# Batch 1's front in the first y phase, regrouped: grouped h tiles, kv and x in one piece each, v1 loaded ahead of the last two w_out rows, and both transpose halves in one PSUM tile

## The chip, the cores and the metric

The kernel runs on one core of a Trainium2 chip. TensorE does its matmuls and transposes and writes the results into a memory called PSUM; VectorE and ScalarE copy them out of it ("evacuate" them), and with GpSimd they convert ("cast") loaded data to bfloat16. The metric is the device time of one execution in microseconds (us), of which less is better. All runs counted here were fast, that is, within 1.5% of the fastest run of their kernel. The profile's span, from the first to the last instruction, is some 1.8 us shorter than the device time (279.9 for 281.66).

## The reference, cut to what matters

```python
# attention without a square matrix, per batch (8) and head (8); seq 576, head size 64
q_s = softmax(q, over head_dim)
k_s = softmax(k, over seq)
kv  = einsum('bhsd,bhse->bhde', k_s, v)
x   = einsum('bhsd,bhde->bhse', q_s, kv)        # -> (4608 tokens, 512)
# then a feed-forward layer with an exact Gelu
h = x @ w_in                                     # 512 -> 2048
out = gelu(h) @ w_out                            # 2048 -> 512
```

Everything is float32 outside; the kernel computes its matmuls in bfloat16.

## The kernel before

The kernel goes through the batches. For each there are five kinds of TensorE work: transposes of the normalised q ("tp"), kv, x, the "h phase" (x times w_in, 16 tiles t of 4 matmuls, each followed by a Gelu on ScalarE), and the "y phase" (Gelu times w_out, 4 token groups j times 16 rows t). The front of batch 1 (tp, kv, x) is fitted in at the end of batch 0's y phase. Up to this point the loads stream in on one queue: q, k, v of batch 0, then w_in in five blocks and w_out in four, with q and k of batch 1 ahead of the last w_out block and v of batch 1 ("v1") behind it.

The kernel's PSUM buffers are three of one bank with tag "h", two "y", one "a", and one of two banks, "a2".

```python
psum_h = tile_pool(bufs=3); psum_y = tile_pool(bufs=2); psum_a = tile_pool(bufs=1)   # in PSUM

def tp_mm(b, half):
    ...
    pool, tag = (psum_h, "h") if half == 1 else (psum_a, "a")
    ps = pool.tile([128, J, 2, 128], BF16, tag=tag)          # one bank each
    st[b][f"tp{half}"] = ps
    ...  # 8 transposes into ps

def tp_step(b, half):
    tp_mm(b, half)
    tp_evac(b, half)                                          # copy to SBUF, VectorE

# loads, all on one queue, in this order
wi = [load_wi(i) for i in range(5)]
wo = [load_wo(i) for i in range(3)]
load_main(1, "q", q, 2)
load_pair(1, "k", k, 2)
wo.append(load_wo(3, 2))                                      # two halves of 512 KB
load_pair(1, "v", v, 4)                                       # four of 288 KB

h_phase(0, {...casts...}, groups={0: 2})       # t=0,1 as a pair, then t by t
...
cast_wo(3, wo[3], 0, 2)                        # VectorE
cast_wo(3, wo[3], 2, 2)                        # VectorE
for hp in range(3):
    cast_v(1, hp, nc.gpsimd)
for t in range(12):
    for j in range(J):
        y_mm(0, yps[j], j, t)
tp_step(1, 0)
tp_step(1, 1)
cast_v(1, 3)                                   # VectorE
load(3)
for t in (12, 13):
    for j in range(J):
        y_mm(0, yps[j], j, t)
kv_mm(1, 0); kv_norm(1, 0, 1)
y_end(0); y_end(1)                             # y_end(j): rows 14 and 15 of group j
y_out(0, yps[0], 0)
x_tile(1, 0, psum_a, "a"); x_tile(1, 1, psum_h, "h")
x_mm(1, 0)
kv_mm(1, 1)
x_evac(1, 0, "s"); x_evac(1, 1, "s")           # "s": ScalarE
kv_norm(1, 1, 2)
y_out(0, yps[1], 1)
y_end(2); y_end(3)
xx = psum_a.tile([128, 2, M], FP32, tag="a2", name="xx")
st[1]["x2"], st[1]["x3"] = xx[:, 0], xx[:, 1]
x_mm(1, 1)
x_evac(1, 2)                                   # VectorE
x_evac(1, 3, "s")                              # ScalarE
...
h_phase(1, ...)
# [...] batches 2 to 7 and the rest follow
```

The softmax here doesn't subtract the row's maximum and nothing guards it: scores larger than these inputs give would overflow.

Of the kernel before, what the change touches and what calls it, by code (L numbers as in the profile page):

```python
# [8 lines left out]
FP32 = mybir.dt.float32  # L9
BF16 = mybir.dt.bfloat16  # L10
# [6 lines left out]
def kernel(  # L17
# [16 lines left out]
    nc = tc.nc  # L34
# [3 lines left out]
    J = 4  # L38
    M = 128 * J
    R = S - M  # L40
    HP = H // 2
    NDM = DM // 128
# [20 lines left out]
    wo_bf = singles.tile([128, NDF, DM], BF16)  # L63
# [17 lines left out]
    st = [dict() for _ in range(B + 1)]  # L81
# [10 lines left out]
    def load_pair(b, name, t, parts=1):  # L92
        f = f32in.tile([128, HP, NS * D], FP32, tag=name + "f")
        st[b][name + "f"] = f
        src = t[b].rearrange("h (p n) d -> (h p) (n d)", n=NS).rearrange("(x q) f -> q x f", q=128)
        n = HP // parts
        for i in range(parts):
            nc.sync.dma_start(out=f[:, i * n:(i + 1) * n, :], in_=src[:, i * n:(i + 1) * n, :])  # L98

    def load(b):  # L100
        load_main(b, "q", q)
        load_pair(b, "k", k)
        load_pair(b, "v", v)
# [40 lines left out]
    def cast_v(b, hp, eng=nc.vector):  # L144
        eng.tensor_copy(  # L145
            out=v_aug[b % 2][:, hp, :, 0:D],
            in_=st[b]["vf"][:, hp, :].rearrange("p (n d) -> p n d", n=NS),
        )
# [5 lines left out]
    def kv_mm(b, half):  # L154


        if "kv" not in st[b]:
            st[b]["kv"] = psum_a.tile([128, 2, 2, 256], FP32, tag="a2", name="kv")
        ps = st[b]["kv"]
        for n in range(NS):  # L160
            for i in range(2):
                for hh in range(2):
                    hp = 2 * half + i
                    pr = slice(hh * 64, hh * 64 + 64)
                    c = slice((hh ^ i) * 64, (hh ^ i) * 64 + 64)
                    nc.tensor.matmul(  # L166
                        ps[c, i, half, 0:D + 1], ek[b % 2][pr, hp, n, :],
                        v_aug[b % 2][pr, hp, n, 0:D + 1], start=(n == 0), stop=(n == NS - 1),
                    )

    def kv_norm(b, h0, h1):

        ps = st[b]["kv"]
        m = h1 - h0
        rec = small.tile([128, 2, 2], FP32, tag="reck")
        nc.vector.reciprocal(rec[:, :, 0:m], ps[:, :, h0:h1, D])
        nc.vector.tensor_tensor(  # L177
            out=kvc[b].rearrange("p (h i) d -> p i h d", i=2)[:, :, h0:h1],
            in0=ps[:, :, h0:h1, 0:D],
            in1=rec[:, :, 0:m].unsqueeze(3).to_broadcast([128, 2, m, D]), op=ALU.mult,  # L180
        )

    def kv_step(b):
        kv_mm(b, 0)
        kv_mm(b, 1)
        kv_norm(b, 0, 2)
# [16 lines left out]
    def tp_mm(b, half):  # L203
        if half == 0:
            st[b]["qT"] = attn_sb.tile([128, J, HP, 128], BF16, tag="qT", name="qT")
        pool, tag = (psum_h, "h") if half == 1 else (psum_a, "a")
        ps = pool.tile([128, J, 2, 128], BF16, tag=tag)
        st[b][f"tp{half}"] = ps
        for i in range(2):
            hp = 2 * half + i  # L210
            for j in range(J):
                nc.tensor.transpose(
                    ps[:, j, i, :],
                    st[b]["eq"][:, j, 2 * hp:2 * hp + 2, :].rearrange("p h d -> p (h d)"),
                    identity,
                )
# [19 lines left out]
    def x_tile(b, hp, pool, tag):  # L236
        if "xT" not in st[b]:
            st[b]["xT"] = attn_sb.tile([128, HP, M], BF16, tag="xT", name="xT")
        st[b][f"x{hp}"] = pool.tile([128, M], FP32, tag=tag, name="ps")
# [32 lines left out]
    def x_evac(b, hp, eng="v"):  # L272
        ps = st[b][f"x{hp}"]
        if eng == "v":
            nc.vector.tensor_copy(out=st[b]["xT"][:, hp, :], in_=ps)  # L275
        else:
            nc.scalar.copy(out=st[b]["xT"][:, hp, :], in_=ps)  # L277

    def h_phase(c, ins, groups={}, pre={}):


        g = moe_sb.tile([128, NDF, M], BF16, tag="g", bufs=1)
        st[c]["g"] = g
        xT = st[c]["xT"]
        t1 = 0
        while t1 < NDF:
            t0, t1 = t1, t1 + groups.get(t1, 1)
            ts = range(t0, t1)
            pss = [psum_h.tile([128, M], FP32, tag="h", name="ps") for t in ts]
            for dm in range(NDM):  # L290
                if t0 == 0:
                    for f in pre.get(dm, []):
                        f()
                for ps, t in zip(pss, ts):
                    nc.tensor.matmul(  # L295
                        ps, wi_bf[:, dm, t * 128:(t + 1) * 128], xT[:, dm, :],
                        start=(dm == 0), stop=(dm == NDM - 1),
                    )
            for ps, t in zip(pss, ts):
                nc.scalar.activation(out=g[:, t, :], in_=ps, func=AF.Gelu)  # L300
                for f in ins.get(t, []):
                    f()

    def y_mm(c, ps, j, t):
        nc.tensor.matmul(  # L305
            ps, st[c]["g"][:, t, j * 128:(j + 1) * 128], wo_bf[:, t, :],
            start=(t == 0), stop=(t == NDF - 1),
        )

    def y_out(c, ps, j):  # L310
        y_sb = moe_sb.tile([128, DM], FP32, tag="y_sb")
        nc.vector.tensor_copy(out=y_sb, in_=ps)  # L312
        if c < B:
            dst = out[c * S:c * S + M, :].rearrange("(p j) n -> p j n", j=J)[:, j, :]
            nc.sync.dma_start(out=dst, in_=y_sb)
        else:
            for b2 in range(2):
                r0 = (2 * j + b2) * S + M
                nc.sync.dma_start(out=out[r0:r0 + R, :], in_=y_sb[b2 * R:(b2 + 1) * R, :])
# [48 lines left out]
    def cast_wi(i, w, eng):  # L368
        n = wi_cols[i]
        r = n // 128  # L370
        o = wi_bf[:, :, wi_off[i]:wi_off[i] + n].rearrange("p d (c m) -> p d c m", c=r)
        w = w[:, :, 0:n].rearrange("p d (m c) -> p d c m", c=r)
        if eng == "p":
            for h in range(2):
                nc.gpsimd.tensor_copy(out=o[:, 2 * h:2 * h + 2], in_=w[:, 2 * h:2 * h + 2])
        else:
            d = NDM // wi_parts[i]
            for c in range(0, NDM, d):
                nc.vector.tensor_copy(out=o[:, c:c + d], in_=w[:, c:c + d])  # L379

    def load_wo(i, parts=1):
        w = wst.tile([128, 4, DM], FP32, tag="w")
        src = moe_w_out[i * 512:(i + 1) * 512, :]
        if i == 0:
            for h in range(2):
                nc.sync.dma_start(
                    out=w[:, 2 * h:2 * h + 2],
                    in_=src[256 * h:256 * h + 256].rearrange("(p c) f -> p c f", c=2),
                )
            return w  # L390
        src = src.rearrange("(p c) f -> p c f", c=4)
        n = 4 // parts
        for h in range(parts):
            nc.sync.dma_start(out=w[:, h * n:(h + 1) * n], in_=src[:, h * n:(h + 1) * n])
        return w

    def cast_wo(i, w, c0=0, n=4):
        nc.vector.tensor_copy(  # L398
            out=wo_bf[:, 4 * i + c0:4 * i + c0 + n, :], in_=w[:, c0:c0 + n]
        )  # L400

    def warm(n, z=zeros):
        ps = psum_y.tile([128, DM], FP32, tag="y")
# [26 lines left out]
    wo = [load_wo(i) for i in range(3)]  # L430
    load_main(1, "q", q, 2)
    load_pair(1, "k", k, 2)
    wo.append(load_wo(3, 2))
    load_pair(1, "v", v, 4)
    load(2)
    nc.vector.memset(zeros32, 0.0)  # L436
    nc.vector.memset(zeros, 0.0)
# [20 lines left out]
    for hp, pool, tag in ((0, psum_y, "y"), (1, psum_y, "y"), (2, psum_a, "a"), (3, psum_h, "h")):  # L458
# [16 lines left out]
        6: [lambda: cast_wi(4, wi[4], "v")],  # L475
        9: [lambda: cast_wo(0, wo[0])],
        12: [lambda: cast_wo(1, wo[1])],
    }, groups={0: 2})


    exp_q(1, parts=2)
# [5 lines left out]
    norm_q(1, 0, 2)  # L487
    norm_q(1, 1, 2, nc.vector)
    cast_wo(3, wo[3], 0, 2)
    cast_wo(3, wo[3], 2, 2)  # L490
    for hp in range(3):
        cast_v(1, hp, nc.gpsimd)
    for t in range(12):
        for j in range(J):
            y_mm(0, yps[j], j, t)
    tp_step(1, 0)
    tp_step(1, 1)
    cast_v(1, 3)
    load(3)
    for t in (12, 13):  # L500
        for j in range(J):
            y_mm(0, yps[j], j, t)

    def y_end(j):
        for t in (14, 15):
            y_mm(0, yps[j], j, t)

    kv_mm(1, 0)
    kv_norm(1, 0, 1)
    y_end(0)  # L510
    y_end(1)
    y_out(0, yps[0], 0)
    x_tile(1, 0, psum_a, "a")
    x_tile(1, 1, psum_h, "h")
    x_mm(1, 0)
    kv_mm(1, 1)
    x_evac(1, 0, "s")
    x_evac(1, 1, "s")
    kv_norm(1, 1, 2)
    y_out(0, yps[1], 1)  # L520
    y_end(2)
    y_end(3)
    xx = psum_a.tile([128, 2, M], FP32, tag="a2", name="xx")
    st[1]["x2"], st[1]["x3"] = xx[:, 0], xx[:, 1]
    x_mm(1, 1)
    x_evac(1, 2)
    x_evac(1, 3, "s")
    y_out(0, yps[2], 2)
    y_out(0, yps[3], 3)
    h_phase(1, {12: [lambda: cast_v_all(2)]}, groups={0: 2})  # L530
# [79 lines left out]
```

## Time and profile before

| | before |
|---|---|
| device time, median of the first 3 runs (us) | 281.54 |
| TensorE busy, share of the span | 97% |
| h phase of batch 0, start to start of y (us) | 15.04 |
| first transpose of batch 1 to its h phase (us) | 6.08 |
| h phase of batch 1 (us) | 14.00 |
| the same phase undisturbed, batch 2 (us) | 13.82 |

The tables and sums of this document go by the starts of TensorE's pieces in the timeline: the start of one piece less the start of the one before. The recorded lengths of the pieces run into one another, because the profile models the ends of matmuls. Two more figures of the kernel before: GpSimd begins its three casts of v1 at 40.52, after a wait for the load, and an undisturbed h phase (batch 2) starts at 76.23 and its y phase at 90.05, so it takes 13.82 us. The lines of "before" on which the main readings rest are in the prediction below.

### The profile page before, as it was taken

The numbers are of one execution on the slowest core, as the hardware profiler recorded it, in microseconds if no ns is written. First come the engines' busy times: TensorE is split into PE (matmuls) and PEld (weight loads), VectorE is DVE, ScalarE is ACT, GpSimd is POOL, SyncE is SP. The second block draws the span as 40 slices with busy tenths as digits, with TensorE's granted clock in tenths as the row PEclk, the third lists the DMA queues.
The fourth block names the chain that finished last, engine by engine and source line by source line (L and its number), as shares of the span: only waits on it lengthen the run. The fifth ranks groups of instructions, "written<-read, shape, count | busy, mean of one in ns | idle before, by whom it ended". The sixth has DMA issues, their size and how long they took to land.

```text
span 279.9 us, 4557 instructions
## 1 busy us (share of the span) xinstructions
PE 271.2 (97%) x1922; PEld 125.6 (45%) x1922; DVE 102.5 (37%) x150; ACT 156.8 (56%) x242; POOL 32.9 (12%) x25
## 2 busy tenths in 40 slices
PE   7689999999999999999999999999999999999995
PEld 3334454444444444444444444444444444444443
DVE  3757496309763530084007500552005200230012
ACT  5756663689466915692469436853683264036400
POOL 1530040002020140005000500050005000000000
PEclk9999999999999999999999999999999999999999
DMA  7999999961994129801991189126501500120033
GB/s 231 385 404 429 399 402 406 400 249 52 283 388 70 40 83 263 332 38 51 237 369 60 40 201 370 67 77 173 129 0 75 150 2 0 75 77 0 0 77 76
DMA packets 44852, 50.10 MB, mean 179 GB/s; under 512 B 20384, under 2 KB 29856, under 8 KB 44576
## 3 DMA queue, kind: packets, MB, share of 16 engines
q1 hardware_dynamic: 44544, 49.68, 53.4%
q8 instruction: 15, 0.25, 0.4%
q10 hardware_dynamic: 288, 0.13, 0.2%
q14 instruction: 5, 0.04, 0.1%
HBM read 36.70 MB, written 9.44 MB: 165 GB/s over the span
## 4 chain that ended last, share of the span: by engine, by line
PE 75%; DMA 20%; ACT 2%; SPq 1%; DVE 0%; ACTq 0%; issue 0%
PE ps L305 36%; PE ps L295 35%; DMA w<-in_moe_w_in_dram 6%; DMA f<-in_k_dram 5%; DMA f<-in_v_dram 4%; DMA out_dram<-y_sb 3%; DMA touch<-in_moe_w_out_dram 2%; PE kv L166 1%; PE ps L327 1%; PE ps L251 1%; ACT ek L138 1%; ACT e L133 1%; ACTq L423 0%; ACT L133 0%; SPq L98 0%; DVE v_aug L145 0%
## 5 line engine op out<-in xcount | busy, mean ns | idle before, releaser
L295 PE MATMUL ps<-xT,wi_bf 128*128 128x512 bf16 x576 | 126.1, 379 | 1.1 <-DVE wi_bf L379 1.0
L305 PE MATMUL ps<-wo_bf,g 128*128 128x512 bf16 x560 | 124.2, 379 | 0.0
L300 ACT ACTIVATE g<-ps 128x512 bf16<-128x512 f32 x144 | 85.6, 597 | 68.5 <-PE ps L295 68.5
L295 PEld LDWEIGHTS <-wi_bf 128*128 128x128 bf16 x576 | 56.1, 98 | 69.4 <-DVE wi_bf L379 1.5
L305 PEld LDWEIGHTS <-g 128*128 128x128 bf16 x560 | 53.9, 98 | 64.3 <-issue 0.4
L312 DVE COPY y_sb<-ps 128x512 f32<-128x512 f32 x35 | 23.9, 686 | 80.6 <-PE ps L305 80.2
L198 POOL TENSOR_TENSOR e<-e,recq 128x2048 bf16<-128x2048 bf16 (+1 forms) x9 | 25.7, 2856 | 177.8 <-DVE recq L197 149.5
L145 DVE CAST v_aug<-f 128x576 bf16<-128x576 f32 x26 | 17.9, 746 | 47.6 <-DMA f<-in_v_dram 47.6
L277 ACT CAST xT<-ps 128x512 bf16<-128x512 f32 x19 | 10.2, 589 | 30.0 <-PE ps L251 20.4
L196 DVE TENSOR_REDUCE qsum<-e 128x16 f32<-128x1024 bf16 (+1 forms) x13 | 21.0, 1615 | 14.8 <-ACT e L133 14.8
L133 ACT ACTIVATE e<-f 128x512 bf16<-128x512 f32 (+1 forms) x42 | 20.5, 556 | 2.0 <-DMA f<-in_q_dram 1.7
L138 ACT ACTIVATE ek<-f 128x2304 bf16<-128x2304 f32 (+1 forms) x10 | 17.2, 1730 | 1.7 <-DMA f<-in_k_dram 1.7
L275 DVE CAST xT<-ps 128x512 bf16<-128x512 f32 x15 | 9.7, 686 | 17.7 <-PE ps L251 14.8
L79 ACT ACT_TABLE_LOAD x9 | 11.5, 1283 | 2.8 <-issue 2.6
L133 ACT ACT_TABLE_LOAD x7 | 9.0, 1283 | 0.1
L405 PE MATMUL ps<-zeros 128*128 128x512 f32 (+1 forms) x14 | 7.6, 686 | 1.5 <-DVE zeros L436 1.5
L379 DVE CAST wi_bf<-w 128x512 bf16<-128x512 f32 (+1 forms) x8 | 7.1, 910 | 2.8 <-DMA w<-in_moe_w_in_dram 2.6
L166 PEld LDWEIGHTS <-ek 64*64 64x64 bf16 x576 | 6.5, 105 | 2.9 <-issue 1.1
L166 PE MATMUL kv<-v_aug,ek 64*64 64x65 bf16 x576 | 7.1, 193 | 0.1
L398 DVE CAST wo_bf<-w 128x2048 bf16<-128x2048 f32 (+1 forms) x5 | 5.1, 1011 | 4.1 <-DMA w<-in_moe_w_out_dram 4.1
L198 DVE TENSOR_TENSOR e<-e,recq 128x1024 bf16<-128x1024 bf16 x4 | 6.4, 1608 | 0.1
L251 PE MATMUL ps<-qT,kvc 64*64 64x512 bf16 x60 | 5.0, 390 | 1.0 <-DVE kvc L177 1.0
(33 smaller groups left out, 41.4 us busy)
## 6 DMA issues: line engine op xcount, KB each, us to landing
out_dram<-y_sb SPq DMA_DIRECT2D x32, 256.0 KB, 2.3
f<-in_k_dram SPq DMA_DIRECT2D x6, 1152.0 KB, 9.8
f<-in_v_dram SPq DMA_DIRECT2D x6, 1152.0 KB, 11.8
f<-in_q_dram SPq DMA_DIRECT2D x6, 1024.0 KB, 7.3
w<-in_moe_w_in_dram SPq DMA_DIRECT2D x6, 512.0 KB, 8.9
f<-in_k_dram SPq DMA_DIRECT2D x4, 576.0 KB, 10.0
f<-in_v_dram SPq DMA_DIRECT2D x8, 288.0 KB, 7.5
f<-in_q_dram SPq DMA_DIRECT2D x4, 512.0 KB, 8.6
```

Of the source, the lines that this page charges most:

```text
L79: nc.scalar.activation(out=scr[:, 1:2], in_=scr[:, 0:1], func=func)
L133: nc.scalar.activation(out=dst[:, i], in_=src[:, u], func=AF.Exp)
L138: nc.scalar.activation(out=ek[b % 2][:, i:i + n], in_=st[b]["kf"][:, i:i + n].rearrange("p x (n d) -> p x n d", n=NS), func=AF.Exp,)
L145: eng.tensor_copy(out=v_aug[b % 2][:, hp, :, 0:D], in_=st[b]["vf"][:, hp, :].rearrange("p (n d) -> p n d", n=NS),)
L166: nc.tensor.matmul(ps[c, i, half, 0:D + 1], ek[b % 2][pr, hp, n, :], v_aug[b % 2][pr, hp, n, 0:D + 1], start=(n == 0), stop=(n == NS - 1),)
L196: nc.vector.reduce_sum(out=qsum, in_=eq[:, :, hs, :], axis=AX.X)
L198: eng.tensor_tensor(out=eq[:, :, hs, :], in0=eq[:, :, hs, :], in1=recq.unsqueeze(3).to_broadcast([128, J, w, D]), op=ALU.mult,)
L277: nc.scalar.copy(out=st[b]["xT"][:, hp, :], in_=ps)
L295: nc.tensor.matmul(ps, wi_bf[:, dm, t * 128:(t + 1) * 128], xT[:, dm, :], start=(dm == 0), stop=(dm == NDM - 1),)
L300: nc.scalar.activation(out=g[:, t, :], in_=ps, func=AF.Gelu)
L305: nc.tensor.matmul(ps, st[c]["g"][:, t, j * 128:(j + 1) * 128], wo_bf[:, t, :], start=(t == 0), stop=(t == NDF - 1),)
L312: nc.vector.tensor_copy(out=y_sb, in_=ps)
```

## The change

The intent: fewer switches between kinds of TensorE work at batch 1's front, v1 early enough for kv in one go, w_out's last rows off VectorE, and no wait for a late cast of w_in in batch 0.

```diff
@@ tp_mm
-        pool, tag = (psum_h, "h") if half == 1 else (psum_a, "a")
-        ps = pool.tile([128, J, 2, 128], BF16, tag=tag)
+        if b == 1:
+            if half == 0:
+                st[b]["tp"] = psum_a.tile([128, 2, J, 2, 128], BF16, tag="a2", name="tp")
+            ps = st[b]["tp"][:, half]
+        else:
+            pool, tag = (psum_h, "h") if half == 1 else (psum_a, "a")
+            ps = pool.tile([128, J, 2, 128], BF16, tag=tag)
@@ h_phase: tiles named in ybanks take one of y's banks
-            pss = [psum_h.tile([128, M], FP32, tag="h", name="ps") for t in ts]
+            pss = []
+            for t in ts:
+                pool, tag = (psum_y, "y") if t in ybanks else (psum_h, "h")
+                pss.append(pool.tile([128, M], FP32, tag=tag, name="ps"))
@@ cast_wi: one cast for each of the four rows, in all blocks
-            d = NDM // wi_parts[i]
-            for c in range(0, NDM, d):
-                nc.vector.tensor_copy(out=o[:, c:c + d], in_=w[:, c:c + d])
+            for c in range(NDM):
+                nc.vector.tensor_copy(out=o[:, c], in_=w[:, c])
[...]
@@ loads
-    wo.append(load_wo(3, 2))
+    wo.append(load_wo(3))            # now its first two rows only
     load_pair(1, "v", v, 4)
+    load_wo_end(wo[3])               # its last two rows, one by one
@@ batch 0
-    }, groups={0: 2})
+    }, groups={0: 2, 4: 4}, ybanks=(6, 8))
@@ batch 1's front
-    cast_wo(3, wo[3], 2, 2)          # VectorE
     [...]
     tp_step(1, 0)
     tp_step(1, 1)
     cast_v(1, 3)
     load(3)
-    [... the order shown above ...]
+    cast_wo(3, wo[3], 2, 1, "s")     # ScalarE
+    y_part(12, range(J))
+    y_part(13, range(J))
+    kv_step(1)                       # both halves, one normalisation
+    cast_wo(3, wo[3], 3, 1, "s")     # ScalarE
+    y_part(14, range(J))
+    y_part(15, (0, 1))
+    y_out(0, yps[0], 0)
+    y_out(0, yps[1], 1)
+    x_tile(1, 0, psum_a, "a")
+    x_tile(1, 1, psum_h, "h")
+    xx = psum_a.tile([128, 2, M], FP32, tag="a2", name="xx")
+    st[1]["x2"], st[1]["x3"] = xx[:, 0], xx[:, 1]
+    x_mm(1, 0)
+    x_mm(1, 1)
+    x_evac(1, 0, "s")
+    x_evac(1, 1, "s")
+    x_evac(1, 2)                     # VectorE
+    x_evac(1, 3)                     # VectorE
+    y_part(15, (2, 3))
     [...]
```

More of the change, by code (lines that the diff above doesn't have):

```diff
@@ L277, in x_evac, with h_phase @@
             nc.scalar.copy(out=st[b]["xT"][:, hp, :], in_=ps)
-    def h_phase(c, ins, groups={}, pre={}):
+    def h_phase(c, ins, groups={}, ybanks=()):
         g = moe_sb.tile([128, NDF, M], BF16, tag="g", bufs=1)
@@ L288, in h_phase @@
             ts = range(t0, t1)
-            pss = [psum_h.tile([128, M], FP32, tag="h", name="ps") for t in ts]
+            pss = []
+            for t in ts:
+                pool, tag = (psum_y, "y") if t in ybanks else (psum_h, "h")
+                pss.append(pool.tile([128, M], FP32, tag=tag, name="ps"))
             for dm in range(NDM):
-                if t0 == 0:
-                    for f in pre.get(dm, []):
-                        f()
                 for ps, t in zip(pss, ts):
@@ L376, in cast_wi, with load_wo @@
         else:
-            d = NDM // wi_parts[i]
-            for c in range(0, NDM, d):
-                nc.vector.tensor_copy(out=o[:, c:c + d], in_=w[:, c:c + d])
-    def load_wo(i, parts=1):
+            for c in range(NDM):
+                nc.vector.tensor_copy(out=o[:, c], in_=w[:, c])
+    def load_wo(i):
         w = wst.tile([128, 4, DM], FP32, tag="w")
@@ L391, in load_wo, with load_wo_end, cast_wo @@
         src = src.rearrange("(p c) f -> p c f", c=4)
-        n = 4 // parts
-        for h in range(parts):
-            nc.sync.dma_start(out=w[:, h * n:(h + 1) * n], in_=src[:, h * n:(h + 1) * n])
-        return w
-    def cast_wo(i, w, c0=0, n=4):
-        nc.vector.tensor_copy(
-            out=wo_bf[:, 4 * i + c0:4 * i + c0 + n, :], in_=w[:, c0:c0 + n]
-        )
+        if i == 3:
+            nc.sync.dma_start(out=w[:, 0:2], in_=src[:, 0:2])
+            return w
+        nc.sync.dma_start(out=w, in_=src)
+        return w
+    def load_wo_end(w):
+        src = moe_w_out[3 * 512:4 * 512, :].rearrange("(p c) f -> p c f", c=4)
+        for c in (2, 3):
+            nc.sync.dma_start(out=w[:, c], in_=src[:, c])
+    def cast_wo(i, w, c0=0, n=4, eng="v"):
+        o, w = wo_bf[:, 4 * i + c0:4 * i + c0 + n, :], w[:, c0:c0 + n]
+        if eng == "v":
+            nc.vector.tensor_copy(out=o, in_=w)
+        else:
+            nc.scalar.copy(out=o, in_=w)
     def warm(n, z=zeros):
@@ L489, with y_part @@
     cast_wo(3, wo[3], 0, 2)
-    cast_wo(3, wo[3], 2, 2)
     for hp in range(3):
         cast_v(1, hp, nc.gpsimd)
+    def y_part(t, js):
+        for j in js:
+            y_mm(0, yps[j], j, t)
     for t in range(12):
-        for j in range(J):
-            y_mm(0, yps[j], j, t)
+        y_part(t, range(J))
     tp_step(1, 0)
@@ L499 @@
     load(3)
-    for t in (12, 13):
-        for j in range(J):
-            y_mm(0, yps[j], j, t)
-    def y_end(j):
-        for t in (14, 15):
-            y_mm(0, yps[j], j, t)
-    kv_mm(1, 0)
-    kv_norm(1, 0, 1)
-    y_end(0)
-    y_end(1)
+    cast_wo(3, wo[3], 2, 1, "s")
[5 more added lines that the diff above has]
+    y_part(15, (0, 1))
     y_out(0, yps[0], 0)
+    y_out(0, yps[1], 1)
     x_tile(1, 0, psum_a, "a")
     x_tile(1, 1, psum_h, "h")
+    xx = psum_a.tile([128, 2, M], FP32, tag="a2", name="xx")
+    st[1]["x2"], st[1]["x3"] = xx[:, 0], xx[:, 1]
     x_mm(1, 0)
-    kv_mm(1, 1)
+    x_mm(1, 1)
     x_evac(1, 0, "s")
     x_evac(1, 1, "s")
-    kv_norm(1, 1, 2)
-    y_out(0, yps[1], 1)
-    y_end(2)
-    y_end(3)
-    xx = psum_a.tile([128, 2, M], FP32, tag="a2", name="xx")
-    st[1]["x2"], st[1]["x3"] = xx[:, 0], xx[:, 1]
-    x_mm(1, 1)
     x_evac(1, 2)
-    x_evac(1, 3, "s")
+    x_evac(1, 3)
+    y_part(15, (2, 3))
     y_out(0, yps[2], 2)
```

## The prediction

> **What bounds the kernel now.** I first read the page's busy shares, then the timeline of each engine for the first 92 us (the change touches nothing later), then the sources and tiles concerned.
>
> ```profile
> PE 271.2 (97%) x1922; PEld 125.6 (45%) x1922; DVE 102.5 (37%) x150; ACT 156.8 (56%) x242; POOL 32.9 (12%) x25
> ```
>
> TensorE is busy 97% of the span, so only stretches where it stands still, or does more than it must, can give time back. The scale comes from its timeline:
>
> ```profile
> 14.63 4.28 PE L295 MATMUL ps<-xT,wi_bf 128*128 128x512 bf16 x19
> 19.95 9.89 PE L295 MATMUL ps<-xT,wi_bf 128*128 128x512 bf16 x45 [1.04 <-DVE wi_bf L379]
> 29.67 10.52 PE L305 MATMUL ps<-wo_bf,g 128*128 128x512 bf16 x48
> 40.03 1.06 PE L212 MATMUL ps<-identity,e 128*128 128x128 bf16 x16
> 40.92 1.89 PE L305 MATMUL ps<-wo_bf,g 128*128 128x512 bf16 x8
> 42.74 0.48 PE L166 MATMUL kv<-v_aug,ek 64*64 64x65 bf16 x36
> 43.16 1.04 PE L305 MATMUL ps<-wo_bf,g 128*128 128x512 bf16 x4
> 44.12 0.41 PE L251 MATMUL ps<-qT,kvc 64*64 64x512 bf16 x4
> 44.36 0.51 PE L166 MATMUL kv<-v_aug,ek 64*64 64x65 bf16 x36
> 44.80 1.04 PE L305 MATMUL ps<-wo_bf,g 128*128 128x512 bf16 x4
> 45.77 0.41 PE L251 MATMUL xx<-qT,kvc 64*64 64x512 bf16 x4
> 46.11 14.16 PE L295 MATMUL ps<-xT,wi_bf 128*128 128x512 bf16 x64
> ```
>
> Columns: start, length, engine, line, instruction, count, idle time before and what ended it. I use start to start. The 48 matmuls from 29.67 to 40.03 take 0.216 us each, 64 take 13.82. One real gap stands between 14.63 and 46.11: 1.04 us at about 18.9, where tile t=4 of batch 0's h phase needs the fourth row of the third w_in block. From 40.03 to 46.11 there is none: 6.08 us of transposes, y, kv and x matmuls, closely packed. Batch 1's v does not hold TensorE up. So the change can win at most about 1 us at the first place and some tenths at the second, of 281.54: under 0.6%.
>
> VectorE's timeline says what ended the gap, and when the next block comes:
>
> ```profile
> 19.28 0.61 DVE L379 CAST wi_bf<-w 128x512 bf16<-128x512 f32 x1 [1.31 <-DMA w<-in_moe_w_in_dram]
> 20.51 2.33 DVE L379 CAST wi_bf<-w 128x1024 bf16<-128x1024 f32 x2 [0.62 <-DMA w<-in_moe_w_in_dram]
> ```
>
> The cast waits for the load, so the stage is fed at DMA speed; the stretch table gives 414 GB/s and a DMA share of 1.04 there. Two casts of 1.08 in 2.33 mean that the second began about 21.76, when its half landed.
>
> The line that decides my forecast stands in the second place, in the timelines of VectorE and ScalarE:
>
> ```profile
> 46.23 0.69 DVE L275 CAST xT<-xx 128x512 bf16<-128x512 f32 x1 [0.20 <-PE xx L251]
> ...
> 46.96 0.59 ACT L277 CAST xT<-xx 128x512 bf16<-128x512 f32 x1 [1.31 <-DVE xT L275]
> ```
>
> The two evacuations read different halves of one two-bank PSUM tile, xx; yet ScalarE began only 0.04 after VectorE ended (46.92). Elsewhere, where each x has its own PSUM tile, VectorE and ScalarE read side by side (73.54 and 73.32) and write the same xT. So it is sharing the PSUM tile that puts the two engines in a row.
>
> **What the Trainium skill says.** "PSUM — Partial Sum Buffer", section "PSUM bank collisions raise a hardware error": two engines must not access one bank and quadrant together, while different banks run clean. The wait on xx is thus no need of the chip, if the halves are the two banks that their sizes say; the trace shows that the program waits all the same. "TensorEngine Tiling (Array Packing)", section "Key Properties": changing the tiling mode drains TensorE. The trace agrees: four y matmuls after kv take 0.96 (43.16 to 44.12) instead of 0.86, eight after the transposes 1.82 instead of 1.73, so about 0.1 a return. "ScalarE: Activation LUTs", section "Table sets: the hidden batching unit": plain copies are in every table set. The trace agrees: at 44.58 ScalarE casts under the Gelu table with no load of a table. The same page, section "What ACT_TABLE_LOAD costs", gives 186 ns + 0.833 per element, so 0.61 us for 512; the trace's casts from PSUM take 0.59.
>
> **The change part by part.**
>
> *h phase of batch 0: four t in one group, one and then t=8 in y's banks.* t=0 to 3 end on TensorE at about 18.09 (14.63 + 16 x 0.216). Then come 12 matmuls (three rows for four t), 2.6 us, before the late fourth row is needed, and its cast is done at 19.89: the 1.04 gap goes. The fourth of the group (t=7) takes the bank of t=3, whose Gelu ends at 18.89, so about 0.2 is lost there; the group ends at about 21.76 (18.95 + 13 x 0.216). Then t=8 needs all rows of the fourth block. Its casts become four of 0.61, some 0.55 apart: rows 2 and 3 land at 21.76 and are cast at 22.37 and 22.92. t=8's last matmul starts at about 22.97 instead of unhindered at 22.4. After it come 28 more: 22.97 + 29 x 0.216 = 29.24. The fifth block is cast by about 25.4, and t=12 wants it at 25.8. Against 29.67: **-0.43**. The rest of the gap moves to the next block, because the load did not get faster.
>
> *v1 ahead of the last two w_out rows, ScalarE casting these.* Rows for t=12, 13 as before. v1 lands some 512 KB / 0.4 = 1.3 us earlier (POOL's first v cast at about 39.2, not 40.52), the last quarter at about 41.4. The w_out rows land at about 42.0 and 42.6, are cast by about 43.3, and are used after 43.9 and 44.8 by the sums below. ScalarE is idle then (4.63 us before 44.58). VectorE loses one cast of 0.69. Off the path: **0**.
>
> *kv, then y 14 and 15, then x, each in one go.* Durations from undisturbed places: kv x72 0.74 (73.32 to 74.06), x x8 0.46 (99.85 to 100.31). After the transposes: y x8 1.82, kv 0.74, y x6 1.30 + 0.10, x 0.46, y x2 0.43 + 0.10 = 4.95. Before: 46.11 - 40.92 = 5.19. **-0.24**: one return to full mode fewer, and joined kv and x.
>
> *The transposes of batch 1 in one two-bank tile a2.* Before, the halves had two PSUM tiles, and 16 transposes took 0.89. Now the first half is written, VectorE reads it, and the second half is written into the same tile. If TensorE is held as ScalarE was on xx, it waits for the whole evacuation. From the first transpose: eight start within 0.39, the last lasts 0.22, VectorE starts at 0.65 (40.03 to 40.68 before), takes 0.69, TensorE goes on at about 1.38 instead of 0.445. **+0.94** on the path, as every later matmul queues behind.
>
> *x evacuation against the next h phase.* Let x start at X. ScalarE has x0 at X + 1.05 and x1 at X + 1.53 (as 44.12 led to 44.58 and 1.07 of work). VectorE first takes two y tiles, from X - 0.1, then x2 and x3, each 0.61 apart: x3 ready at X + 2.42. The first matmul needing it would be ready at X + 0.99 + 6 x 0.216 = X + 2.29: a wait of 0.19 with hand-over. Before, 64 matmuls took 14.00 there instead of 13.84, so 0.16 was lost already. **+0.03**.
>
> Sum: -0.43 - 0.24 + 0.94 + 0.03 = **+0.30**, so 281.84; I say 281.8.
>
> **The rivals.** *No wait on the shared tile*: TensorE writes bank two while VectorE reads bank one. For it: nothing on the chip forbids that, and whoever made the tile may have meant it. Against it: the wait of ScalarE on xx. Then the sum is -0.64: 280.9. *The gap disappears whole*, if VectorE's finer casts keep pace or the loads land a little earlier: a further 0.5 less, so 281.3, or 280.4 with the first rival; against it speaks that the load is at 414 GB/s already. *The w_out rows or v1 come late*: the margin of the last cast is over 1 us when transposes stall, and some 0.6 when they don't; 2 KB runs instead of 4 KB may slow the loads, and every us of that beyond the margin shows in full: 282 to 283. *The gain in front is hidden by the loads of batch 1*: exp of q1 starts when its load lands (33.06, 1.31 idle), whatever TensorE did. But the normalised q is ready at 38.97, and the transposes would start at 39.6, so 0.6 is to spare.
>
> **Range and chances.** I give the shared-tile wait five chances in six, so 281.8 is the centre, and the range must still reach the other outcome: 280.8 to 282.2. Every route stays within 1% of 281.54, hence almost all chance on "within 2%".
>
> **What would show it.** In TensorE's timeline of the changed kernel: no wait at t=4, a wait of some 0.5 for the wi_bf cast at t=8, and y of batch 0 starting at about 29.24. The transposes as two groups of eight, with some 0.9 idle between them whose releaser is VectorE's qT copy (wrong if 16 run together). kv as one piece of 72 near 43.2, h of batch 1 near 46.3. ScalarE casting wo_bf twice, each about 0.6, with TensorE waiting for neither. After 60 us the pattern of before, shifted by +0.3. I would be wrong, above all, if the halves of the shared tile were not held apart.

## The result, and the profile after

The changed kernel took 281.89 us (median of 6 runs, 281.34 to 283.15), the one before 281.61 (6 runs, 281.27 to 282.06). The ratio is 1.0011, with a 95% interval of 0.9989 to 1.0033. A ratio here is the mean time of one kernel's fast runs over the mean of the other's in the same rounds, so not quite the ratio of the medians. The totals alone say only that the two are equal within their noise. The traces say why.

TensorE's timeline of the changed kernel, in the columns start, length, engine, line, instruction, count, and in brackets the idle time before it and what ended that (the "releaser"). Line numbers have moved: L300 is the h matmul, L310 y, L217 the transposes, L256 x.

```profile
14.75 14.70 PE L300 MATMUL ps<-xT,wi_bf 128*128 128x512 bf16 x64
29.29 10.52 PE L310 MATMUL ps<-wo_bf,g 128*128 128x512 bf16 x48
39.65 0.61 PE L217 MATMUL tp<-identity,e 128*128 128x128 bf16 x8
41.05 0.61 PE L217 MATMUL tp<-identity,e 128*128 128x128 bf16 x8 [0.78 <-DVE qT L226]
41.49 1.89 PE L310 MATMUL ps<-wo_bf,g 128*128 128x512 bf16 x8
43.31 0.78 PE L166 MATMUL kv<-v_aug,ek 64*64 64x65 bf16 x72
44.02 1.47 PE L310 MATMUL ps<-wo_bf,g 128*128 128x512 bf16 x6
45.42 0.41 PE L256 MATMUL ps<-qT,kvc 64*64 64x512 bf16 x4
45.66 0.39 PE L256 MATMUL xx<-qT,kvc 64*64 64x512 bf16 x4
45.98 0.60 PE L310 MATMUL ps<-wo_bf,g 128*128 128x512 bf16 x2
46.51 14.03 PE L300 MATMUL ps<-xT,wi_bf 128*128 128x512 bf16 x64
60.38 6.42 PE L310 MATMUL ps<-wo_bf,g 128*128 128x512 bf16 x29
```

The reader is to see three things. The 1.04 gap of the first line of before is gone, and y starts 14.54 after h instead of 15.04. The transposes are two pieces now, with 0.78 idle between them and VectorE's qT copy named as what ended it; from the first of them to h it is 6.86 instead of 6.08. And kv and x are one piece each.

VectorE's and ScalarE's parts of it:

```profile
40.30 0.69 DVE L226 COPY qT<-tp 128x1024 bf16<-128x1024 bf16 x1 [0.66 <-PE tp L217]
41.69 0.69 DVE L226 COPY qT<-tp 128x1024 bf16<-128x1024 bf16 x1 [0.70 <-PE tp L217]
42.30 0.74 DVE L145 CAST v_aug<-f 128x576 bf16<-128x576 f32 x1
```

```profile
42.12 1.24 ACT L412 CAST wo_bf<-w 128x512 bf16<-128x512 f32 x2 [2.13 <-DMA w<-in_moe_w_out_dram]
```

TensorE starts its second half at 41.05, when VectorE's first copy has ended (40.30 + 0.69 = 40.99): the two engines take turns on the tile. GpSimd's first cast of v1, which waits for the load, begins 1.18 us earlier than before (39.34 against 40.52). ScalarE casts both w_out rows by 43.36, and row 14 is first used at 44.02.

In batch 0's h phase the wait has not gone altogether. The weight loads of TensorE ("PEld") that waited, between 20 and 26 us:

```profile
22.50 0.10 PEld L300 LDWEIGHTS <-wi_bf 128*128 128x128 bf16 x1 [0.53 <-DVE wi_bf L383]
23.02 2.92 PEld L300 LDWEIGHTS <-wi_bf 128*128 128x128 bf16 x15 [0.42 <-DVE wi_bf L383]
```

Two waits of 0.53 and 0.42 for the casts of the fourth block are where t=8 stands. They are idle time of the weight load; of TensorE's time the phase still loses 14.54 - 13.82 = 0.72. Of that, 0.20 is not the casts' doing: in profiles without any wait at t=8 the phase takes 14.02. The weight loads show one more idle time, 0.32 up to 19.07, just behind the end of t=3's Gelu (19.02), whose bank t=7 takes.

After 60 us the pattern is that of before, shifted: the y phase of batch 1 starts at 60.38 instead of 60.11, so 0.27 later, and of that 0.12 was there at the start of batch 0's h phase already (14.75 against 14.63).

### The profile page after: what moved, and what is told of

It is laid out like the page before. It is cut to its first block, busy times and chain, and to the rows that moved or that the text cites. A ratio compares the mean times of both kernels' runs of the same rounds, so it can differ in the third digit from the quotient of the medians.

```text
span 280.1 us, 4564 instructions
## 1 busy us (share of the span) xinstructions
PE 271.0 (97%) x1922; PEld 125.2 (45%) x1922; DVE 102.2 (37%) x152; ACT 157.0 (56%) x243; POOL 33.0 (12%) x25
## 4 chain that ended last, share of the span: by engine, by line
PE 75%; DMA 18%; SPq 2%; ACT 2%; ACTq 0%; issue 0%; DVE 0%
PE ps L310 36%; PE ps L300 35%; DMA w<-in_moe_w_in_dram 6%; DMA f<-in_v_dram 4%; DMA w<-in_moe_w_out_dram 3%; DMA out_dram<-y_sb 3%; SPq L98 2%; DMA touch<-in_moe_w_out_dram 2%; PE kv L166 1%; PE ps L332 1%; PE ps L256 1%; ACT ek L138 1%; ACT e L133 1%; ACTq L435 0%; ACT L133 0%
## 5 line engine op out<-in xcount | busy, mean ns | idle before, releaser
L300 PE MATMUL ps<-xT,wi_bf 128*128 128x512 bf16 x576 | 126.4, 379 | 0.2
L310 PE MATMUL ps<-wo_bf,g 128*128 128x512 bf16 x560 | 124.2, 379 | 0.0
L300 PEld LDWEIGHTS <-wi_bf 128*128 128x128 bf16 x576 | 56.1, 98 | 69.0 <-DVE wi_bf L383 1.0
L310 PEld LDWEIGHTS <-g 128*128 128x128 bf16 x560 | 54.0, 98 | 64.6 <-issue 0.8
L383 DVE CAST wi_bf<-w 128x512 bf16<-128x512 f32 x12 | 7.4, 660 | 2.5 <-DMA w<-in_moe_w_in_dram 2.2
L256 PE MATMUL ps<-qT,kvc 64*64 64x512 bf16 x60 | 5.0, 390 | 1.0 <-DVE kvc L177 1.0
L410 DVE CAST wo_bf<-w 128x2048 bf16<-128x2048 f32 (+1 forms) x4 | 4.4, 1090 | 3.8 <-DMA w<-in_moe_w_out_dram 3.8
```

The source lines that it names most:

```text
L300: nc.tensor.matmul(ps, wi_bf[:, dm, t * 128:(t + 1) * 128], xT[:, dm, :], start=(dm == 0), stop=(dm == NDM - 1),)
L310: nc.tensor.matmul(ps, st[c]["g"][:, t, j * 128:(j + 1) * 128], wo_bf[:, t, :], start=(t == 0), stop=(t == NDF - 1),)
```

## The experiments

Theory: TensorE stands still for about 0.9 us because the program lets the second half of the transposes wait for the read of the first, and it does so because both halves share one PSUM tile; this eats what the other parts win. Rival one: the second half waits for something else (its q, or VectorE's other work). Rival two: the gain of batch 0's groups gets lost on the way, to late loads. Eleven more runs were made, two of them repeats, in three sets, each set on one chip with its own runs of the kernel before. All gave correct results. Stage times come from one profile each. The ratios are to the kernel before in the same set, whose median was 281.50 in the first set (two tiles, both halves first, ScalarE evacuates, old groups), 281.71 in the second (changed again; before, shared tile; two tiles, late v; two tiles, pair at 8) and 281.39 in the third (two tiles again; two tiles, pair, v cast in two; changed, pair at 8).

| kernel | h to y, batch 0 | first tp to h, batch 1 | median (us) | ratio to before, 95% interval |
|---|---|---|---|---|
| before | 15.04 | 6.08 | 281.61 | |
| changed | 14.54 | 6.86 | 281.89 | 1.0011 (0.9989 to 1.0033) |
| changed, again | 14.27 | 6.85 | 281.61 | 1.0001 (0.9988 to 1.0015) |
| two tiles | 14.02 | 6.22 | 280.65 | 0.9972 (0.9960 to 0.9984) |
| two tiles, again | 14.59 | 5.91 | 280.76 | 0.9978 (0.9965 to 0.9990) |
| both halves first | 14.03 | 6.32 | 280.95 | 0.9989 (0.9967 to 1.0012) |
| ScalarE evacuates | 14.24 | 7.18 | 281.85 | 1.0027 (1.0003 to 1.0051) |
| old groups | 14.69 | 6.86 | 281.76 | 1.0016 (0.9993 to 1.0038) |
| before, shared tile | 14.78 | 7.02 | 282.23 | 1.0025 (1.0013 to 1.0038) |
| two tiles, late v | 14.33 | 6.84 | 281.58 | 1.0001 (0.9988 to 1.0013) |
| two tiles, pair at 8 | 14.02 | 5.91 | 280.64 | 0.9970 (0.9957 to 0.9982) |
| two tiles, pair, v cast in two | 14.02 | 5.91 | 280.80 | 0.9975 (0.9962 to 0.9989) |
| changed, pair at 8 | 14.02 | 6.85 | 281.52 | 1.0003 (0.9989 to 1.0016) |

### A tile for each half

```diff
-            if half == 0:
-                st[b]["tp"] = psum_a.tile([128, 2, J, 2, 128], BF16, tag="a2", name="tp")
-            ps = st[b]["tp"][:, half]
+            ps = psum_a.tile([128, J, 2, 128], BF16, tag="a" if half == 0 else "a2", name="tp")
```

> The changed kernel, but batch 1's two transpose halves get a one-bank PSUM tile each. Theory (TensorE is held only because both halves share one PSUM tile): the 16 transposes run together in about 0.89 us from first to next matmul instead of 1.84, the later work moves 0.9 earlier, kv starts at about 42.4 instead of 43.3, total about 281.0, that is 0.9 below the changed kernel and 0.6 below the one before. Rival (the second half waits for something else, such as its normalised q or VectorE's speed): the gap of 0.8 stays and the time too.

TensorE's timeline of this kernel, from its transposes to its h phase:

```profile
39.05 1.06 PE L215 MATMUL tp<-identity,e 128*128 128x128 bf16 x16
39.95 1.89 PE L308 MATMUL ps<-wo_bf,g 128*128 128x512 bf16 x8
41.77 1.02 PE L166 MATMUL kv<-v_aug,ek 64*64 64x65 bf16 x72
42.79 1.46 PE L308 MATMUL ps<-wo_bf,g 128*128 128x512 bf16 x5
```

(This trace lacks the record of one of the six y matmuls of the last line.) The 16 transposes run together, 0.90 from the first to the next matmul instead of 1.84: the whole 0.94 is back. But from the first transpose to h it takes 6.22, only 0.64 less than in the changed kernel. The 72 kv matmuls fill 1.02 (41.77 to 42.79) instead of 0.71, and VectorE's timeline shows for what:

```profile
41.51 0.75 DVE L145 CAST v_aug<-f 128x576 bf16<-128x576 f32 x1 [0.52 <-DMA f<-in_v_dram]
```

VectorE had nothing to do and waited for the last quarter of v1, which was cast only at 42.26, when kv was already under way. A wait that the stall had covered came out. The profiled execution is 1.24 below the changed kernel's (280.66 and 281.90), more than the stage gives: 0.52 comes from the earlier part, where this run had no wait at t=8 (14.02 instead of 14.54), and 0.08 from an earlier start of h. Whether that belongs to the program was tested by a second run.

### The same kernel again

No edit.

> The two-tile kernel unedited, a second time. Its first run had the fourth w_in block cast from 19.8 and no wait at t=8, where the changed kernel had 20.2 to 20.6 and 0.7 to 0.95. Theory (when the loads land is chance of the run, not of the program): this time it may be late, with a wait of up to 0.7 at t=8 and a total of 280.7 to 281.2; transposes to h of batch 1 stay at 6.0 to 6.3. Rival (the two-tile program itself gets its loads earlier): 19.6 to 19.8 and 280.6 again.

The loads came late this time. VectorE's casts of the fourth and fifth w_in blocks (eight pieces), first in the earlier run, then in this one:

```profile
19.78 4.90 DVE L381 CAST wi_bf<-w 128x512 bf16<-128x512 f32 x8 [1.25 <-DMA w<-in_moe_w_in_dram]
```

```profile
20.55 4.92 DVE L381 CAST wi_bf<-w 128x512 bf16<-128x512 f32 x8 [0.62 <-DMA w<-in_moe_w_in_dram]
```

One program, 0.77 us apart. The two runs were on two chips, but that is not needed for such a difference: in the first set, on one chip, three kernels that are alike up to this point cast the fourth block from 19.78 (two tiles), 19.56 (both halves first) and 20.27 (ScalarE evacuates). h to y took 14.59 here, and the weight loads waited 0.58 and 0.43 at t=8: so the wait at t=8 goes with the landing of the loads, not with the two tiles. And from the first transpose to h it is 5.91, 0.95 below the changed kernel, because TensorE came to kv later (42.33) and v1 was ready. The two waits are in part for one and the same stream of loads: what TensorE does not lose at t=8 it can lose at kv. The two profiled executions show it: they are 0.27 apart (280.66 and 280.93), which is about what the two stages add up to (+0.57 and -0.31). The stage of 5.91 lies just below the expected 6.0 to 6.3. Why the loads land early or late stays open.

### Both halves written before either is read

```diff
-    tp_step(1, 0)
-    tp_step(1, 1)
+    tp_mm(1, 0)
+    tp_mm(1, 1)
+    tp_evac(1, 0)
+    tp_evac(1, 1)
```

> The changed kernel with the shared tile kept, but both halves are written before either is read. Theory (a wait of write after read on the shared tile, by order of the program): the gap of 0.8 us goes, because no read stands between the two writes; VectorE's first evacuation starts some 0.4 later (about 40.7), nothing else waits; total about 281.0, as with two tiles. Rival (sharing a tile costs by itself, in any order): 281.9.

The tile is still shared, and the gap is gone all the same:

```profile
38.96 1.06 PE L217 MATMUL tp<-identity,e 128*128 128x128 bf16 x16
39.85 1.89 PE L310 MATMUL ps<-wo_bf,g 128*128 128x512 bf16 x8
41.67 0.51 PE L166 MATMUL kv<-v_aug,ek 64*64 64x65 bf16 x38
42.33 0.47 PE L166 MATMUL kv<-v_aug,ek 64*64 64x65 bf16 x34 [0.15 <-DVE v_aug L145]
```

So sharing by itself cost no stall here. What costs is the order write, read, write. VectorE's first copy starts at 40.05, 1.09 after the first transpose instead of 0.65, which nothing waits for. The wait for v1 shows here as such, 0.15 in the middle of kv. The totals (0.9989, with one run at 282.73) are too wide to tell this kernel from the one before; the trace decides. One thing no run shows: the two halves of the shared tile written and read at the same time. That they lie in two different banks follows from their sizes and from no trace; and what part of the software puts the wait in was not looked at.

### A slower reader of the first half

```diff
-    tp_step(1, 0)
+    tp_mm(1, 0)
+    tp_evac(1, 0, "s")
```

with the second half as it was.

> The changed kernel with the first half evacuated by ScalarE instead of VectorE: the same copy took ScalarE 0.99 us in batch 0 and takes VectorE 0.69. Theory (TensorE waits out the whole evacuation): the gap before the second half grows by 0.3, from 0.78 to about 1.08, and the total to about 282.2. Rival (TensorE waits for VectorE's queue, not for the reader of the tile): the gap shrinks or goes.

TensorE's second half and ScalarE's copy:

```profile
41.06 0.61 PE L217 MATMUL tp<-identity,e 128*128 128x128 bf16 x8 [1.10 <-ACT qT L228]
```

```profile
40.00 1.01 ACT L228 COPY qT<-tp 128x1024 bf16<-128x1024 bf16 x1 [0.33 <-PE tp L217]
```

The copy took 1.01 instead of 0.69, the gap grew from 0.78 to 1.10, both by 0.32, and its releaser is now ScalarE. The stall follows the reader's whole length, for both readers tried. VectorE's queue has no part in it. The total (281.85) missed the expected 282.2, as y began 14.24 after h here, 0.30 earlier than in the first run of the changed kernel.

### The shared tile alone, in the kernel before

```diff
-        pool, tag = (psum_h, "h") if half == 1 else (psum_a, "a")
-        ps = pool.tile([128, J, 2, 128], BF16, tag=tag)
+        [... as in the change ...]
```

> The kernel before with this part of the change alone: batch 1's transposes in one shared two-bank tile. Theory: the gap of 0.8 us between the halves appears, transposes to h of batch 1 grow from 6.08 to about 6.9 to 7.0, total 0.8 to 0.9 above the kernel before (about 282.4). Rival (in the old order of work a later wait swallows it, for instance TensorE's wait for v or for x): below 0.4 more.

```profile
39.86 0.61 PE L217 MATMUL tp<-identity,e 128*128 128x128 bf16 x8
41.25 0.61 PE L217 MATMUL tp<-identity,e 128*128 128x128 bf16 x8 [0.78 <-DVE qT L226]
```

The stage grew from 6.08 to 7.02, by 0.94. The ratio is 1.0025, clear of 1, some 0.7 us; the set's runs of the kernel before had a median of 281.71, so the medians differ by 0.52. That is less than the 0.8 to 0.9 expected, but the interval reaches from 0.4 to 1.1 us, and h of batch 1 starts 0.77 later in the profile (46.88 for 46.11) although the earlier part took 0.26 less. So no later wait swallows it.

### Batch 0's groups as before

```diff
-    }, groups={0: 2, 4: 4}, ybanks=(6, 8))
+    }, groups={0: 2})
```

> The changed kernel with batch 0's h phase as before: tiles one by one after the first two, none in y's banks; everything else as changed. Theory: the gap of about 1.0 us at t=4 is back, y of batch 0 starts about 0.4 later (29.7 instead of 29.3), total about 282.3. Rival (the group's gain is lost later, because batch 1's q is set by its load): y starts later, but h of batch 1 at 46.5 as now and the total 281.9.

```profile
14.79 4.27 PE L300 MATMUL ps<-xT,wi_bf 128*128 128x512 bf16 x18
19.76 9.89 PE L300 MATMUL ps<-xT,wi_bf 128*128 128x512 bf16 x44 [0.69 <-DVE wi_bf L383]
```

The gap at t=4 is back, 0.69 here. The total missed the expected 282.3 and could not show it (281.76, against 281.89 and 281.61 of the changed kernel): the loads' chance is as large as the effect. Runs with equally late loads can be compared, by the start of the fourth block's cast: 20.17 here and 20.24 in the second run of the changed kernel, 14.69 against 14.27 for the phase, so 0.42; 20.51 before and 20.56 in its first run, 15.04 against 14.54, so 0.50. h of batch 1 starts at 46.70 here and at 46.17 in that second run, 0.10 of it from an earlier start of h in batch 0, so the gain reaches it; for the changed kernel the second rival falls.

### The changed kernel again

No edit.

> The changed kernel unedited, a second time, on the chip of the three other runs of this set. Theory: the wait at t=8 of batch 0 depends on when the loads of w_in land, which differs from run to run; it can be anything from 0 to 1 us here, while the gap of 0.78 us between the transposes stays to within 0.05. Total 281.3 to 282.0. Rival (the load's lateness belongs to this program, and the earlier landing to the two-tile program): the fourth w_in block is cast from 20.5 again.

The fourth block was cast from 20.24, the weight loads waited 0.25 and 0.44, h to y took 14.27, and the gap between the transposes was 0.78 once more. The total was 281.61 with a ratio of 1.0001. The stall is fixed in the program, and the wait at t=8 is not.

### v1 late again, with two tiles

```diff
     load_pair(1, "k", k, 2)
     wo.append(load_wo(3))
-    load_pair(1, "v", v, 4)
     load_wo_end(wo[3])
+    load_pair(1, "v", v, 4)
```

on top of the two-tile kernel.

> The two-tile kernel, with v1 loaded after all of w_out as before the change; ScalarE still casts the last two w_out rows. Theory (with the stall on the shared tile gone, the landing of v1's last quarter sets kv): the quarter lands 512 KB at 0.4 MB per us, 1.3 us later, at about 42.8, kv ends about 1.2 later than in the two-tile kernel, total about 281.9. Rival (v1's order is hidden anyway, as in the kernel before): 280.7 as the two-tile kernel.

```profile
42.02 0.69 PE L166 MATMUL kv<-v_aug,ek 64*64 64x65 bf16 x38
43.26 0.48 PE L166 MATMUL kv<-v_aug,ek 64*64 64x65 bf16 x34 [0.54 <-DVE v_aug L145]
43.67 1.47 PE L308 MATMUL ps<-wo_bf,g 128*128 128x512 bf16 x6
```

kv now takes 1.65 (42.02 to 43.67), and the stage takes 6.84, as long as with the shared tile (6.86). The last quarter of v1 was cast from 42.45, after a wait of 1.21 for its load; kv ended 0.9 later than in the two-tile run, not 1.2 as expected. The total, 281.58, is that of the kernel before. So the earlier v1 is worth up to 0.9 us (6.84 against 5.91), but only once the stall is away. That it is worth nothing in the changed kernel was not run, but worked out: a v1 this late would be cast by 43.20, and kv starts at 43.31 or 42.97 there, with its second half some 0.35 later. The kernel before with the shared tile, where v1 is late too, agrees: VectorE took v1's last quarter at 42.50 without a wait for its load.

### t=8 and t=9 as a pair

```diff
-    }, groups={0: 2, 4: 4}, ybanks=(6, 8))
+    }, groups={0: 2, 4: 4, 8: 2}, ybanks=(6, 8))
```

once on the two-tile kernel, once on the changed kernel.

> The two-tile kernel, with t=8 and 9 of batch 0 as a pair, so that two matmuls of other rows stand before each wait for a cast of the fourth w_in block. Theory: where the loads land late (casts of it from 20.5), the wait of up to 0.95 us at t=8 falls below 0.2, y of batch 0 starts 13.9 to 14.1 after h; where they land early there is nothing to win. Total 280.4 to 280.7. Rival (the wait moves on to t=12): y starts 14.3 or more after h, total as the two-tile kernel with late loads, about 281.1.

> The changed kernel, shared tile and all, with t=8 and 9 of batch 0 as a pair. Theory: with the fourth w_in block cast from 20.2 to 20.6 the wait at t=8 falls from 0.7 to 0.95 to below 0.3 and y of batch 0 starts 13.9 to 14.1 after h; the gap of 0.78 between the transposes stays; total 281.2 to 281.4. Rival (the wait moves to a later tile): y starts 14.3 to 14.5 after h and the total is 281.6 to 281.9.

On two tiles the loads came early (cast from 19.68), so this run could not tell anything about the pair: 14.02, as the two-tile kernel in its early run. On the changed kernel they came as late as they ever did, and the pair did its work:

```profile
20.57 4.91 DVE L383 CAST wi_bf<-w 128x512 bf16<-128x512 f32 x8 [0.63 <-DMA w<-in_moe_w_in_dram]
```

```profile
14.86 14.19 PE L300 MATMUL ps<-xT,wi_bf 128*128 128x512 bf16 x62
28.88 10.52 PE L310 MATMUL ps<-wo_bf,g 128*128 128x512 bf16 x47
```

14.02 instead of 14.54 with equally late casts (20.57 and 20.56), and no wait of the weight loads at t=8. The total (281.52, expected 281.2 to 281.4) lies within the noise of the changed kernel's two medians, so the half microsecond is shown for the stage and not for the whole.

### Two tiles, the pair, and v1's last cast in two pieces

```diff
-    cast_v(1, 3)
+    for n0, n1 in ((0, 5), (5, NS)):
+        nc.vector.tensor_copy(
+            out=v_aug[1][:, 3, n0:n1, 0:D],
+            in_=st[1]["vf"][:, 3, :].rearrange("p (n d) -> p n d", n=NS)[:, n0:n1],
+        )
```

> The two-tile kernel with t=8 and 9 of batch 0 paired and VectorE's cast of v1's last quarter in two pieces (5 and 4 of its 9 rows), so that kv's second half can begin after the first piece. Theory: no wait at t=8 whatever the loads do, and the wait of some 0.28 for v1 inside kv falls below 0.1; transposes to h of batch 1 5.9 to 6.0, total 280.2 to 280.6. Rival (both waits are gone already in runs with early loads): 280.6 as the paired kernel.

The stage is 5.91 and h to y 14.02, both without a wait; v1's last cast began at 41.02 here, earlier than in the two-tile run that waited (41.51), so it is not shown that the two pieces were needed. The median of 280.80 (280.29 to 281.02) is missed by 0.2 and is no better than that of two tiles alone. All four runs of kernels with two tiles and early v1 lie 0.22% to 0.30% below the kernel before, with intervals that exclude 1. None of their executions took longer than 281.09, and none of the changed kernel's was shorter than 281.30, so they are below both kernels; which of them is best these runs don't tell.

## Why the prediction was right

The total was forecast at 281.8 and came out at 281.89 and, in the second set, 281.61. The totals can't confirm the forecast shift of +0.30: the median was 0.28 above the kernel before the first time and 0.10 below it the second time, both within the noise. What speaks for the prediction is the stages.

- **The gap at t=4 goes, a wait at t=8 takes its place.** Right in kind. Forecast -0.43; -0.50 and -0.42 where loads were equally late. y of batch 0 began at 29.29, 0.05 from the forecast 29.24, though h itself began 0.12 later than assumed. The forecast 0.2 for t=3's bank is there as well (14.02 less 13.82). But the size depends on the run: the cast of the fourth block started between 19.56 and 20.57 in these profiles. The prediction's rival "the gap disappears whole" took place where loads came early (two tiles, first run, and both halves first: 14.02 and 14.03, no wait at t=8). In five profiles, these two among them, the third block was cast whole by 18.9 at the latest, so that the old order would hardly have had its gap at t=4 either. So the -0.43 belongs to late loads, and that the changed kernel's first profile had them, as the one forecast from, is luck.
- **v1 and the two w_out rows: nothing.** Right. GpSimd's first v cast came at 39.34 (forecast 39.2), ScalarE's casts took 0.62 each and were done by 43.36 (forecast 43.3), and no one waited for them. Without the stall it is not so: in the first two-tile run kv took 1.02 instead of 0.71, because v1's last quarter was cast only from 41.51 (the forecast landing was 41.4). The rival without a stall has no term for that.
- **kv and x in one go.** Forecast -0.24 from the end of the transposes to h (5.19 to 4.95); measured 5.02, so -0.17. The term for x was too small: 0.46 forecast, 0.56 measured (45.42 to 45.98). The forecast took it from a place where kv follows x; four x matmuls took 0.24 before kv and 0.34 before h in the prediction's own lines. Its reading of the 0.1 "a return" to full mode is not safe either: the eight y matmuls after the transposes are 0.09 longer as well, and the transposes run at 128*128 like y, so no tiling mode changes there.
- **The shared tile.** Forecast +0.94, with five chances in six. The transposes took 1.84 instead of 0.89 to 0.90, so +0.94 to +0.95. Two tiles, another order, and a slower reader show the cause from three sides. The hint was the one line of the kernel before in which ScalarE waited for VectorE on xx. There one reader waits for another, here a writer for a reader; that the one implies the other was a guess, which came true.
- **x evacuation.** Forecast +0.03; the h phase of batch 1 took 13.87 (46.51 to 60.38) instead of 14.00, so -0.13. VectorE had x3 ready at 47.79, just when it was needed, so a wait of some 0.05 was left instead of the 0.19 forecast. (The prediction sets 13.84 beside the 14.00 of before; by its own figure it should be 13.82, so 0.18 was lost there and its term is +0.01.) About 0.1 of the difference is the longer x above, that is, the boundary between the two terms.
- **The sum.** The terms measured in the first profile, -0.50 + 0.95 - 0.17 - 0.13 = +0.15, and the later start of batch 0's h phase (+0.12) give +0.27, which is the shift at 60.38. The forecast was +0.30; a part of the agreement is luck, for the +0.12 is in no term of it.
- **The rival without the stall** put its time at 280.9. The kernels that remove the stall, with v1 early, were at 280.64 to 280.95; with v1 late it was 281.58.

## What to carry to other kernels

Two halves of a buffer that are written by one engine and read by another should be two tiles, or both be written before the first is read; otherwise the writer may stand still for the reader's whole length, even if its own data are ready. Look for such turns in the trace of the kernel at hand before trusting a new shared tile: one wait of an engine for another that only reads the same tile is hint enough to test it. And when a stall is removed, expect the next load behind it to show: here v1's early load was worth up to 0.9 us without the stall and, as far as the traces tell, nothing with it.

## What the Trainium skill lacked or had wrong

- "PSUM — Partial Sum Buffer", section "PSUM bank collisions raise a hardware error", tells what the chip forbids: two engines on one bank and quadrant. It does not warn that a program may take turns on a tile of two banks as well. Here that cost 0.94 us of TensorE's time, for a tile whose halves are one bank each by size, while separate one-bank tiles ran side by side: VectorE read the first half from 39.70 while the 16 transposes went on from 39.05 to 39.95 without a gap.
- "TensorEngine Tiling (Array Packing)", section "Key Properties", says that a change of tiling mode drains TensorE and gives no figure. Here the six y matmuls after kv (64*64 to 128*128) took 1.40 us instead of 1.30. But eight y matmuls after the transposes, which are 128*128 too, took 1.82 instead of 1.73, so the runs don't show that the change of mode is what costs the 0.1.
- "DMA: Bandwidth & Descriptors" gives rates and latencies and nothing on how far the landing of a queued load moves between runs of one program. Here a cast that waits for its load began at 19.78 in one run and at 20.55 in another of the same program on another chip, 0.77 us apart, and 0.71 apart between two kernels that are alike up to there on one chip (19.56 and 20.27), which is as much as most of the effects studied.
